# Strassen's scheme for y @ w2_in: the reads of a PSUM bank are given out after both products of the bank

## Chip, cores and metric

One Trainium2 chip, one of its cores. The metric is the device time of one execution in microseconds; the median of the runs is compared.

## What is computed

The input goes through an attention with a small state (its result is called x below, 4352 rows of 512), then through two feed-forward layers. The change touches the second of them only, `_moe2_ref`, with 512 inputs, 2048 hidden columns and 512 outputs per row:

```python
def _moe_ref(x, w_in, w_out, g_ln):
    ...
    return (ln @ w_out)

def _moe2_ref(x, w_in, w_out):
    h = x @ w_in
    r = np.maximum(h, 0.0)
    g = r * r
    return (g @ w_out)

def reference(**kwargs):
    ...
    x = _moe_ref(x=x, **moe_kwargs)          # this result is y below
    return _moe2_ref(x=x, **moe2_kwargs)     # y @ w2_in, relu squared, @ w2_out
```

## The kernel before

Everything is float32. A product of full precision is made of three matmuls (`PASSES`): each operand is split into a high part (a cast to `float32r`) and a rest, and high by high, high by rest and rest by high are added up in PSUM.

**Two phases.** The first does attention and the first feed-forward layer and leaves its result, y, in DRAM. The second, from `p1.close()` on (line 964), does y @ w2_in, the squared relu and the product with w2_out. Its rows come in nine groups j: eight of 512 rows, and the ninth (`j == B`) of 256. For each group, m runs over eight pieces of the hidden dimension, 256 columns each. One pair (j, m) is a step; `emit_l3(j, m)` (line 1010) makes the hidden piece, and `emit_l4(j, m)` (line 1068) multiplies it by w2_out and adds it to four output banks. The loop at line 1096 emits `emit_l3` of a step, the load of the weights of the step after next (`load_wa`), then `emit_l4` of the step before. So TensorE's order is: hidden piece of step i, output part of step i-1, hidden piece of step i+1, output part of step i. In each group from the second on, the output banks of the group before are copied out (`osb`, on ScalarE and VectorE in turn) during its first two steps.

**Strassen's scheme.** For the eight groups of 512 rows, `emit_l3` makes the hidden piece (two by two blocks) from seven products instead of eight, in Winograd's form. `PRODUCTS` (line 23) lists them in the order P1, P6, P2, P7, P5, P3, P4. A product is six matmuls of 256 columns (two k by three passes, `product`, line 1001). Two products share one bank of PSUM (`h2`, a pool of four banks): P1 and P6 the first, P2 and P7 the second, P5 and P3 the third, P4 the fourth alone. Seven reads combine them: a copy `u1` of P1 on ScalarE (`copy`, line 250), and on VectorE (`plus`, line 985) `u2 = u1 + P6`, `c11 = u1 + P2`, `u3 = u2 + P7`, `u4 = u2 + P5`, `c22 = u3 + P5`, `c12 = u4 + P3`, `c21 = u3 - P4`. The four c blocks are the tile `r`. `squares` (line 989) then squares (`L993`, VectorE), casts (`L250`, ScalarE) and subtracts (`L256`, VectorE) each half of r into the tile `g`, which `emit_l4` reads. The ninth group uses no such scheme: it makes its blocks straight, 24 matmuls to one bank, and one read of the full bank.

**What sets the order.** Each engine takes its instructions in the order in which the program emits them. A planner, `Flow`, decides at emission when a read goes out: `fl.pe(cost, ...)` advances a modelled time before every three matmuls, and `fl.poll` emits those waiting tasks whose operands the model holds to be ready. So a read spawned behind P1 goes out between the two k of P6. The framework orders accesses to a tile by their order of emission, and here a tile of PSUM is a whole bank: a read emitted after some matmuls of the bank waits for all of them, and matmuls of the same bank emitted behind the read wait for the read.

**Beside this, early in the second phase,** w2_out is still being decoded: 512 KB loads (`raw`, a ring of three), a conversion on ScalarE (`L300`), two operations on VectorE (`L303`, `L306`), then the split into `wb`, with its cast on ScalarE and its subtraction on GpSimd or VectorE (`L256`). In the fifth to eighth step of each group, y of the next group is loaded and split for the seven products (`yt`, `sy`). All loads and stores are issued by SP in program order; `load_wa` is one load of 1792 KB per step into two buffers `wa`.

Of the kernel before, what the change touches and what calls it, by code (L numbers as in the profile page):

```python
# [153 lines left out]
def attn_solu_relu2_kernel(  # L154
# [92 lines left out]
    def copy(out, in_):  # L247
        def emit(e):
            if e == "A":
                nc.scalar.copy(out=out, in_=in_)  # L250
            else:
                eng_of[e].tensor_copy(out=out, in_=in_)
        return emit
# [11 lines left out]
    def one(engs, emit):  # L265

        def gen(f):
            f = yield engs, f, emit
            return f
        return fl.spawn(gen(fl.end + 0.15), 0.0)  # L270
# [703 lines left out]
    def then(engs, emit, *tasks):  # L974

        at = fl.end + 0.15

        def gen():
            yield None, 0.0, lambda: all(t["done"] is not None for t in tasks)
            f = yield engs, max([at] + [t["done"] for t in tasks]), emit  # L980
            return f
        return fl.spawn(gen(), 0.0)

    def plus(out, in0, in1, *tasks, op=ALU.add):
        return then({"V": 0.42}, lambda e: nc.vector.tensor_tensor(  # L985
            out=out, in0=in0, in1=in1, op=op
        ), *tasks)

    def squares(r, g, tasks):

        def gen():
            yield None, 0.0, lambda: all(t["done"] is not None for t in tasks)
            f = yield {"V": 0.69}, max(t["done"] for t in tasks), lambda e: nc.vector.scalar_tensor_tensor(  # L993
                out=r, in0=r, scalar=0.0, in1=r, op0=ALU.max, op1=ALU.mult
            )
            f = yield {"A": 0.62}, f, copy(g[:, 0], r)
            f = yield {"V": 0.69}, f, sub(g[:, 1], r, g[:, 0].bitcast(F32))
            return f
        return fl.spawn(gen(), 0.0)

    def product(ps, j, w, a, waits, first=True, last=True):
        for k in range(2):
            fl.pe(0.36, *waits)
            for i, (x, y) in enumerate(PASSES):
                nc.tensor.matmul(  # L1005
                    out=ps, lhsT=w[:, y, k], rhs=a[:, x, k],
                    start=(first and k == 0 and i == 0), stop=(last and k == 1 and i == 2),
                )

    def emit_l3(j, m):  # L1010
        w = wa.pop((j, m))
        ready = done.pop(("wa", j, m))
        if m == 0:
            fl.mark(done["y", j], fl.end)
        g = gp.tile([P, 2, 2, S], F32R, tag="g", name="g")
        r = gp.tile([P, 2, 2, Q], F32, tag="r", name="r")
        gt[j, m] = g
        if j == B:
            bank_ = ph2.tile([P, 2, Q], F32, tag="h2", name="h2")
            slot = h2_free.pop(0)  # L1020
            for h in range(2):
                for k in range(2):
                    fl.need(done["y", j, k])
                    product(
                        bank_[:, h], j, w[:, W_AT[f"B{k + 1}{h + 1}"]], yt[j, k],
                        (slot, ready, done["y", j, k]), k == 0, k == 1,
                    )
            first = one({"A": 0.57}, lambda e: nc.scalar.activation(  # L1028
                out=r[:, 0], in_=bank_, func=AF.Relu
            ))  # L1030
            h2_free.append(first)
            done["g", j, m] = squares(r[:, 0], g[:, :, :, :Q], [first])
            return
        u1, u2, u3, u4 = (gp.tile([P, Q], F32, tag=n, name=n, bufs=1) for n in ("u1", "u2", "u3", "u4"))
        ps, t, slots = {}, {}, {}
        for n, (p, a, b) in enumerate(PRODUCTS):
            if n % 2 == 0:
                bank_ = ph2.tile([P, 2, Q], F32, tag="h2", name="h2")
                slot = h2_free.pop(0)
            ps[p] = bank_[:, n % 2]  # L1040
            fl.need(done["y", j, a])
            product(
                ps[p], j, w[:, W_AT[b] - 1], yt[j, a],
                (slot, ready, done["y", j, a]),
            )
            if p == "P1":
                t["u1"] = one({"A": 0.34}, copy(u1, ps["P1"]))
            if p == "P6":
                t["u2"] = plus(u2, u1, ps["P6"], t["u1"])
            if p == "P2":  # L1050
                t["c11"] = plus(r[:, 0, 0], u1, ps["P2"], t["u1"])
            if p == "P7":
                t["u3"] = plus(u3, u2, ps["P7"], t["u2"])
            if p == "P5":
                t["u4"] = plus(u4, u2, ps["P5"], t["u2"])
                t["c22"] = plus(r[:, 1, 1], u3, ps["P5"], t["u3"])
            if p == "P3":
                t["c12"] = plus(r[:, 1, 0], u4, ps["P3"], t["u4"])
            if p == "P4":
                t["c21"] = plus(r[:, 0, 1], u3, ps["P4"], t["u3"], op=ALU.subtract)  # L1060
        for users in (("u1", "u2"), ("c11", "u3"), ("u4", "c22", "c12"), ("c21",)):
            h2_free.append([t[u] for u in users])
        done["g", j, m] = [
            squares(r[:, h].rearrange("p i t -> p (i t)"), g[:, :, h], [t[c] for c in cs])
            for h, cs in ((1, ("c12", "c22")), (0, ("c11", "c21")))
        ]
# [29 lines left out]
    for i in range(len(steps) + 1):  # L1096
        if i < len(steps):
            j, m = steps[i]
            if m == 4 and j < B:
                load_y(j + 1)  # L1100
            emit_l3(j, m)
            if i + 2 < len(steps):
                load_wa(*steps[i + 2])
        if i:
            emit_l4(*steps[i - 1])
# [55 lines left out]
```

## Time and profile before

| | us |
|---|---|
| median of 3 runs | 1290.7 |
| lowest, highest | 1290.64, 1294.53 |
| the profiled execution | 1295.02 |
| its span (first to last instruction) | 1292.9 |
| TensorE matmuls busy | 1162.2 (90%) |
| VectorE busy | 743.0 (57%) |
| ScalarE busy | 458.8 (35%) |
| GpSimd busy | 156.0 (12%) |
| the 16 DMA engines | 46% busy, 166 GB/s on average |
| second phase, TensorE's first hidden matmul to that of the ninth group | 426.75 to 1238.39 |

The time of an execution is that from outside, the span that of the instructions; 2.1 us lie around the span. Busy time of an engine is a sum over its instructions; for TensorE neighbouring matmuls overlap, so a stretch in which it never waits is seen by the starts of its matmuls and by missing waits, not by the busy share.

### The profile page before, as it was taken

The page shows a single profiled execution, that of the slowest core. Times are in us where ns is not written, and L with a number is a line of the kernel's source. Part 1 is how long each engine was busy: PE and PEld are TensorE (multiplying, and loading weights), DVE is VectorE, ACT ScalarE, POOL GpSimd, SP SyncE. Part 2 cuts the span into 40 slices and gives each one's busy share as a digit, 9 for nine tenths or more (in the row PEclk, how much of TensorE's full clock was granted, in tenths as well). Part 3 has the DMA queues.
Part 4 walks back from the last instruction along what each step waited for, and adds up shares of the span by engine and source line. Part 5 has one row for each costly group of instructions (what it writes and reads, how often), then busy time and mean ns, then how long its engine had stood idle before and what let it go on. Part 6 is the DMA issues. An engine that isn't in the chain of part 4 may idle for free.

```text
span 1292.9 us, 17901 instructions
## 1 busy us (share of the span) xinstructions
PE 1162.2 (90%) x7144; PEld 954.4 (74%) x7144; DVE 743.0 (57%) x1429; ACT 458.8 (35%) x848; POOL 156.0 (12%) x209
## 2 busy tenths in 40 slices
PE   5799999999999889888889889889888989888898
PEld 1477777777777877777777777778777777777787
DVE  6876887778765776345536445436445545544432
ACT  5866777777655442112112112112112112111112
POOL 1522343442332130000000000000000000000000
PEclk8899999999999999999999989999999999999999
DMA  9223425532464674544444435445354445353343
GB/s 357 85 72 137 152 99 199 197 125 96 152 220 182 229 284 157 193 159 158 165 185 158 159 121 198 142 176 192 126 183 168 171 147 204 121 197 135 142 163 114
DMA packets 42691, 214.02 MB, mean 166 GB/s; under 512 B 4976, under 2 KB 14192, under 8 KB 31344
## 3 DMA queue, kind: packets, MB, share of 16 engines
q1 hardware_dynamic: 42608, 212.88, 46.0%
q8 instruction: 56, 0.92, 0.3%
q14 instruction: 27, 0.22, 0.1%
HBM read 178.26 MB, written 34.60 MB: 165 GB/s over the span
## 4 chain that ended last, share of the span: by engine, by line
PE 61%; DVE 5%; ACT 3%; DMA 2%; issue 2%; POOL 0%; ACTq 0%; SPq 0%; DVEq 0%
PE h L1005 29%; PE o L1078 27%; PE y L682 3%; DVE u L985 2%; ACT u L250 2%; DVE r L985 2%; DMA out<-osb 2%; PE hps L621 1%; DMA raw<-w_in 0%; PE lnTp L647 0%; DMA raw<-w_out 0%; DVE u L586 0%; DVE dec L303 0%; DVE dec L306 0%; DVE lt L656 0%
## 5 line engine op out<-in xcount | busy, mean ns | idle before, releaser
L1005 PE MATMUL h<-yt,wa 128*128 128x256 f32 x2880 | 402.0, 289 | 98.3 <-DVE r L985 36.4
L1005 PEld LDWEIGHTS h<-yt,wa 128*128 128x128 f32 x2880 | 364.8, 191 | 139.1 <-DVE r L985 47.5
L1078 PE MATMUL o<-wb,g 128*128 128x512 f32 x1632 | 385.0, 391 | 0.0
L1078 PEld LDWEIGHTS o<-wb,g 128*128 128x128 f32 x1632 | 302.9, 189 | 60.2
L985 DVE TENSOR_TENSOR u<-u,h 128x256 f32<-128x256 f32 x192 | 80.6, 420 | 275.2 <-PE h L1005 275.0
L250 ACT CAST g<-r 128x512 fp32r<-128x512 f32 x136 | 84.5, 623 | 390.7 <-DVE r L993 390.7
L682 PE MATMUL y<-lt,wo 128*128 128x512 f32 (+1 forms) x864 | 218.0, 393 | 3.1 <-ACT lt L653 2.3
L682 PEld LDWEIGHTS y<-lt,wo 128*128 128x128 f32 x864 | 149.1, 190 | 39.7 <-issue 5.9
L985 DVE TENSOR_TENSOR r<-u,h 128x256 f32<-128x256 f32 x256 | 100.6, 417 | 69.2 <-PE h L1005 69.2
L993 DVE SCALAR_TENSOR_TENSOR r<-r 128x512 f32<-128x512 f32 x136 | 93.0, 690 | 32.5 <-ACT r L1028 29.4
L256 DVE TENSOR_TENSOR g<-r,g 128x512 fp32r<-128x512 f32 x136 | 93.4, 692 | 10.5 <-ACT g L250 6.4
L621 PE MATMUL hps<-sw,aT 128*128 128x512 f32 x368 | 97.5, 413 | 0.2 <-ACT s_sb L356 0.2
L250 ACT COPY u<-h 128x256 f32<-128x256 f32 x64 | 23.8, 372 | 189.3 <-PE h L1005 189.1
L621 PEld LDWEIGHTS hps<-sw,aT 128*128 128x128 f32 x368 | 68.8, 189 | 23.7 <-issue 6.3
L656 DVE SCALAR_TENSOR_TENSOR lt<-lnTp,g_sb,lt 128x512 fp32r<-128x512 f32 (+1 forms) x72 | 51.4, 713 | 26.1 <-ACT lt L653 25.3
L557 DVE TENSOR_REDUCE hm<-hps 128x1 f32<-128x512 f32 x68 | 45.9, 686 | 26.3 <-PE hps L621 20.5
L250 ACT COPY u<-hps 128x512 f32<-128x512 f32 x68 | 39.0, 583 | 41.7 <-DVE hm L557 40.0
L653 ACT ACTIVATE lt<-lnTp,g_sb 128x512 fp32r<-128x512 f32 (+1 forms) x72 | 48.1, 670 | 5.0 <-PE lnTp L647 4.9
L586 DVE SCALAR_TENSOR_TENSOR u<-u,e 128x1024 f32<-128x1024 f32 x34 | 44.4, 1306 | 8.4 <-ACT e L581 8.2
L592 ACT ACTIVATE e<-u,nmu 128x1024 f32<-128x1024 f32 x34 | 39.2, 1152 | 12.6 <-DVE nmu L589 12.6
L647 PE MATMUL lnTp<-ident,u 128*128 128x128 f32 x272 | 41.6, 273 | 1.5 <-DVE a_sb L256 1.4
L581 ACT ACTIVATE e<-u,nmx 128x1024 f32<-128x1024 f32 x34 | 39.2, 1152 | 6.8 <-DVE nmx L574 5.8
(92 smaller groups left out, 840.7 us busy)
## 6 DMA issues: line engine op xcount, KB each, us to landing
wa<-w_d SPq DMA_DIRECT2D x64, 1792.0 KB, 7.3
w_d<-w2s SPq DMA_DIRECT2D x32, 512.0 KB, 2.9
raw<-w_out SPq DMA_DIRECT2D x24, 512.0 KB, 6.2
out<-osb SPq DMA_DIRECT2D x34, 256.0 KB, 5.4
xT<-x_t SPq DMA_DIRECT2D x8, 1024.0 KB, 5.2
xn<-x_n SPq DMA_DIRECT2D x8, 1024.0 KB, 6.4
y_d<-ys SPq DMA_DIRECT2D x16, 512.0 KB, 4.0
raw<-w_in SPq DMA_DIRECT2D x16, 512.0 KB, 5.9
```

The lines of the kernel that those rows point to most:

```text
L250: nc.scalar.copy(out=out, in_=in_)
L256: return lambda e: eng_of[e].tensor_tensor(out=out, in0=in0, in1=in1, op=ALU.subtract)
L557: one({"V": 0.68}, lambda e, c=c, ps=ps: nc.vector.tensor_reduce(out=m2[:, c:c + 1], in_=ps, axis=AX.X, op=ALU.max)),
L586: nc.vector.scalar_tensor_tensor(out=u, in0=u, scalar=1.0, in1=e_, op0=ALU.mult, op1=ALU.mult, accum_out=us)
L621: nc.tensor.matmul(out=ps, lhsT=lhsT(i, k), rhs=rhs(j, k)[:, cs], start=(k == 0 and n == 0), stop=(k == n_k - 1 and n == len(passes) - 1),)
L653: f = yield {"A": 0.1 + nt * 0.143}, f, lambda e: nc.scalar.activation(out=o[:, 0], in_=pf, func=AF.Copy, scale=gk)
L656: f = yield {"V": 0.1 + nt * 0.155}, f, lambda e: nc.vector.scalar_tensor_tensor(out=o[:, 1], in0=pf, scalar=gk, in1=o[:, 0].bitcast(F32), ...
L682: nc.tensor.matmul(out=ps, lhsT=wo[k][:, w, c * P:(c + 1) * P], rhs=o[:, a], start=(k == 0 and i == 0), stop=(k == K1 - 1 and i == 2),)
L985: return then({"V": 0.42}, lambda e: nc.vector.tensor_tensor(out=out, in0=in0, in1=in1, op=op), *tasks)
L993: f = yield {"V": 0.69}, max(t["done"] for t in tasks), lambda e: nc.vector.scalar_tensor_tensor(out=r, in0=r, scalar=0.0, in1=r, op0=ALU. ...
L1005: nc.tensor.matmul(out=ps, lhsT=w[:, y, k], rhs=a[:, x, k], start=(first and k == 0 and i == 0), stop=(last and k == 1 and i == 2),)
L1078: nc.tensor.matmul(out=ops[j][t], lhsT=g[:, a, h, t * P:(t + 1) * P], rhs=wb[m + h * M2][:, w, :], start=(m == 0 and h == 1 and i == 0), s ...
```

## The change

In `emit_l3`, the seven reads are given out at other places of the loop over the products. Before, each was given out right behind the product that it reads. Now `u1` and `u2` are given out behind P6, `u3` and `c11` behind P7, `c22`, `u4` and `c12` behind P3, `c21` behind P4 as before. So all reads of a bank are spawned behind the last matmul to that bank, and within a bank the order of the reads is changed (u3 ahead of c11, c22 ahead of u4). The planned cost of the copy is 0.36 where it was 0.34. Number and kind of instructions are the same; no matmul changes its place among the matmuls.

```diff
-            if p == "P1":
-                t["u1"] = one({"A": 0.34}, copy(u1, ps["P1"]))
+
             if p == "P6":
+                t["u1"] = one({"A": 0.36}, copy(u1, ps["P1"]))
                 t["u2"] = plus(u2, u1, ps["P6"], t["u1"])
-            if p == "P2":
-                t["c11"] = plus(r[:, 0, 0], u1, ps["P2"], t["u1"])
             if p == "P7":
                 t["u3"] = plus(u3, u2, ps["P7"], t["u2"])
-            if p == "P5":
+                t["c11"] = plus(r[:, 0, 0], u1, ps["P2"], t["u1"])
+            if p == "P3":
+                t["c22"] = plus(r[:, 1, 1], u3, ps["P5"], t["u3"])
                 t["u4"] = plus(u4, u2, ps["P5"], t["u2"])
-                t["c22"] = plus(r[:, 1, 1], u3, ps["P5"], t["u3"])
-            if p == "P3":
                 t["c12"] = plus(r[:, 1, 0], u4, ps["P3"], t["u4"])
             if p == "P4":
                 t["c21"] = plus(r[:, 0, 1], u3, ps["P4"], t["u3"], op=ALU.subtract)
```

TensorE, the hidden piece of one step in the second group, before (h_5628, h_5642, h_5657 and h_5672 are its four banks in turn; the square brackets name the engines that a matmul waits for):

```order
L1005 MATMUL h_5628<-yt,wa 128x256 [waits DMAHW1_49]
L1005 MATMUL h_5628<-yt,wa 128x256 x8
L1005 MATMUL h_5628<-yt,wa 128x256 [waits Activation_49]
L1005 MATMUL h_5628<-yt,wa 128x256 x2
L1005 MATMUL h_5642<-yt,wa 128x256 x9
L1005 MATMUL h_5642<-yt,wa 128x256 [waits DVE_49]
L1005 MATMUL h_5642<-yt,wa 128x256 x2
L1005 MATMUL h_5657<-yt,wa 128x256 x9
L1005 MATMUL h_5657<-yt,wa 128x256 [waits DVE_49]
L1005 MATMUL h_5657<-yt,wa 128x256 x2
L1005 MATMUL h_5672<-yt,wa 128x256 x6
```

The same step of the changed kernel (its banks are h_5628, h_5641, h_5656, h_5671):

```order
L1005 MATMUL h_5628<-yt,wa 128x256 [waits DMAHW1_49,DVE_49]
L1005 MATMUL h_5628<-yt,wa 128x256 x11
L1005 MATMUL h_5641<-yt,wa 128x256 [waits DVE_49]
L1005 MATMUL h_5641<-yt,wa 128x256 x11
L1005 MATMUL h_5656<-yt,wa 128x256 [waits DVE_49]
L1005 MATMUL h_5656<-yt,wa 128x256 x11
L1005 MATMUL h_5671<-yt,wa 128x256 [waits DVE_49]
L1005 MATMUL h_5671<-yt,wa 128x256 x5
```

The wait ahead of the tenth matmul of each of the first three banks is gone; instead the first matmul of each bank waits, for the reads of the same bank by the step before.

VectorE, the reads of that step and what follows, before:

```order
L985 TENSOR_TENSOR u_5625<-u_5624,h_5628 128x256 [waits PE_49,Activation_49]
L985 TENSOR_TENSOR r<-u_5624,h_5642 128x256 [waits PE_49]
L985 TENSOR_TENSOR u_5626<-u_5625,h_5642 128x256 [waits DVE_49,PE_49]
L985 TENSOR_TENSOR u_5627<-u_5625,h_5657 128x256 [waits PE_49]
L985 TENSOR_TENSOR r<-u_5626,h_5657 128x256 [waits DVE_49,PE_49]
L985 TENSOR_TENSOR r<-u_5627,h_5657 128x256 [waits DVE_49]
L993 SCALAR_TENSOR_TENSOR r<-r 128x512 [waits DVE_49]
L985 TENSOR_TENSOR r<-u_5626,h_5672 128x256 [waits PE_49]
L993 SCALAR_TENSOR_TENSOR r<-r 128x512 [waits DVE_49]
L256 TENSOR_TENSOR g<-r,g 128x512 [waits Activation_49] x2
```

And of the change:

```order
L985 TENSOR_TENSOR u_5625<-u_5624,h_5628 128x256 [waits Activation_49]
L985 TENSOR_TENSOR u_5626<-u_5625,h_5641 128x256 [waits DVE_49,PE_49]
L985 TENSOR_TENSOR r<-u_5624,h_5641 128x256
L985 TENSOR_TENSOR r<-u_5626,h_5656 128x256 [waits DVE_49,PE_49]
L985 TENSOR_TENSOR u_5627<-u_5625,h_5656 128x256
L985 TENSOR_TENSOR r<-u_5626,h_5671 128x256 [waits PE_49]
L985 TENSOR_TENSOR r<-u_5627,h_5656 128x256 [waits DVE_49]
L993 SCALAR_TENSOR_TENSOR r<-r 128x512 [waits DVE_49] x2
L256 TENSOR_TENSOR g<-r,g 128x512 [waits Activation_49] x2
```

One wait for TensorE per bank is left; c21 (of the fourth bank, h_5671) now stands ahead of c12, and both squarings behind the two of them.

ScalarE at the start of the second phase, before (u_4575 and u_4643 are the copies u1 of the first two steps, raw the pieces of w2_out):

```order
L250 COPY u_4575<-h_4579 128x256 [waits PE_49]
L300 ACTIVATE dec<-raw 128x512 [waits DMAHW1_49]
L300 ACTIVATE dec<-raw 128x512 [waits DMAHW2_49,Activation_49]
L250 COPY u_4643<-h_4647 128x256 [waits DVE_49,PE_49,Activation_49]
L250 CAST g<-r 128x512 [waits DVE_49]
L300 ACTIVATE dec<-raw 128x512 [waits DMAHW3_49,Pool_49]
```

And of the change:

```order
L250 COPY u_4575<-h_4579 128x256 [waits PE_49]
L300 ACTIVATE dec<-raw 128x512 [waits DMAHW1_49]
L300 ACTIVATE dec<-raw 128x512 [waits DMAHW2_49,Activation_49]
L300 ACTIVATE dec<-raw 128x512 [waits DMAHW3_49,Pool_49]
L250 COPY u_4641<-h_4645 128x256 [waits DVE_49,PE_49,Activation_49]
L250 CAST g<-r 128x512 [waits DVE_49] x2
```

The third decode, with its wait for a load, now stands ahead of the copy of the second step and of both casts of the first.

## Rows read from the trace of the kernel before

**Rows 1.** Waits, 426.7 to 1238.4 us: waiter, releaser, us in total, times, longest.
```profile
PE h L1005 <- DVE r L985: 36.4, 55, 1.8
PE h L1005 <- ACT u L250: 33.7, 64, 1.1
PE h L1005 <- DVE u L985: 28.3, 55, 0.5
```

**Rows 2.** Timeline of one step: start us, us, engine, line, instruction, [idle before <-releaser].
```profile
816.23 1.23 PE L1005 MATMUL h<-yt,wa 128*128 128x256 f32 x9
...
817.98 1.69 PE L1005 MATMUL h<-yt,wa 128*128 128x256 f32 x12 [0.52 <-ACT u L250]
...
820.18 1.70 PE L1005 MATMUL h<-yt,wa 128*128 128x256 f32 x12 [0.51 <-DVE r L985]
...
822.39 1.33 PE L1005 MATMUL h<-yt,wa 128*128 128x256 f32 x9 [0.51 <-DVE u L985]
...
823.56 5.63 PE L1078 MATMUL o<-wb,g 128*128 128x512 f32 x24
...
825.50 1.46 DVE L256 TENSOR_TENSOR g<-r,g 128x512 fp32r<-128x512 f32 x2
...
829.03 1.23 PE L1005 MATMUL h<-yt,wa 128*128 128x256 f32 x9
```

**Rows 3.** Timeline, TensorE alone, a step with two waits, to the next's start.
```profile
791.41 1.23 PE L1005 MATMUL h<-yt,wa 128*128 128x256 f32 x9
...
796.80 1.34 PE L1005 MATMUL h<-yt,wa 128*128 128x256 f32 x9 [0.51 <-DVE u L985]
...
803.44 1.23 PE L1005 MATMUL h<-yt,wa 128*128 128x256 f32 x9
```

**Rows 4.** Timeline, TensorE alone, a step with one wait, to the next's start.
```profile
484.00 1.23 PE L1005 MATMUL h<-yt,wa 128*128 128x256 f32 x9
485.69 4.22 PE L1005 MATMUL h<-yt,wa 128*128 128x256 f32 x33 [0.46 <-ACT u L250]
...
495.22 1.23 PE L1005 MATMUL h<-yt,wa 128*128 128x256 f32 x9
```

**Rows 5.** Timeline, TensorE alone, the ninth group's first step and the second's start.
```profile
1238.39 3.04 PE L1005 MATMUL h<-yt,wa 128*128 128x256 f32 x24
1241.27 5.63 PE L1078 MATMUL o<-wb,g 128*128 128x512 f32 x24
1246.73 3.04 PE L1005 MATMUL h<-yt,wa 128*128 128x256 f32 x24
```

**Rows 6.** Timeline, TensorE alone, the second phase's first hidden and first output matmuls.
```profile
426.75 1.24 PE L1005 MATMUL h<-yt,wa 128*128 128x256 f32 x9
...
439.83 2.46 PE L1078 MATMUL o<-wb,g 128*128 128x512 f32 x10
```

**Rows 7.** Timeline, ScalarE alone, the first two decodes of that phase.
```profile
431.51 0.67 ACT L300 ACTIVATE dec<-raw 128x512 f32<-128x512 f32 x1 [3.11 <-DMA raw<-w_out]
433.44 0.68 ACT L300 ACTIVATE dec<-raw 128x512 f32<-128x512 f32 x1 [1.26 <-DMA raw<-w_out]
```

**Rows 8.** Windows: stretch, length, busy us (instructions) of PE PEld DVE ACT POOL, PEclk, DMA share, GB/s.
```profile
426.70:532.80 106.10, 94.37 (x572) 82.49 (x572) 73.26 (x138) 36.30 (x65) 17.62 (x13) 1.00 0.64 231
532.80:634.80 102.00, 89.52 (x530) 77.38 (x529) 50.75 (x101) 18.00 (x33) 0.00 (x0) 1.00 0.46 165
...
736.80:841.80 105.00, 92.42 (x530) 79.80 (x529) 50.74 (x101) 18.00 (x33) 0.00 (x0) 0.97 0.45 160
...
1238.40:1288.60 50.20, 50.20 (x312) 45.34 (x311) 12.38 (x18) 11.42 (x19) 0.00 (x0) 1.00 0.43 147
```

**Rows 9.** Tile wa, loads of 427 to 1238 us, from issue to landing.
```profile
DMA to landing us min/median/max: 5.0/7.3/8.8
```

**Rows 10.** Timeline, second step of the sixth group: a wait behind the output copies.
```profile
947.42 0.69 DVE L252 COPY osb<-o 128x512 f32<-128x512 f32 x1 [5.27 <-PE h L1005]
...
948.82 1.69 PE L1005 MATMUL h<-yt,wa 128*128 128x256 f32 x12 [1.79 <-DVE r L985]
```

## The prediction

> **What bounds the kernel now.** I read the waits of the second phase first. TensorE's hidden matmuls wait 174 times, 98.4 us in all, and every time for a read of PSUM: 64 times for the copy u1, 55 for an r block (mostly c11), 55 for a u (u4) [rows 1]. The groups of output matmuls never wait. Then the timeline of a common step [rows 2]: TensorE runs nine matmuls, stands idle 0.52 us for ScalarE, runs twelve, idle 0.51 for VectorE, twelve, idle 0.51, then nine and the 24 output matmuls without a gap. The breaks lie where the order puts the waits, ahead of the tenth matmul of a bank: P1's or P2's or P5's read goes out in the middle of the bank's second product, waits for the nine matmuls so far, and the last three wait for it. In the steady steps nothing else ends a wait of TensorE, so the phase is TensorE's time plus these waits.
>
> **What one wait costs** is more than its idle time, since matmuls overlap and a restart is slow. The trace has its own experiment, steps in which the planner happened to give out fewer reads in mid-bank. From the start of one step to the next: three waits 829.03 - 816.23 = 12.80 us [rows 2], two waits 803.44 - 791.41 = 12.03 (ScalarE's stands in the line left out) [rows 3], one wait 495.22 - 484.00 = 11.22 [rows 4]. That is 0.77 to 0.81 per wait, and puts a step without waits near 10.45.
>
> **What a step without waits costs**, independently: the ninth group reads only full banks and has no wait. There 24 hidden matmuls take 1241.27 - 1238.39 = 2.88 us, 0.120 each, and 24 output matmuls 1246.73 - 1241.27 = 5.46 us [rows 5]. A Strassen step has 42 and 24: 42 x 0.120 + 5.46 = 10.50. The two ways agree, and I take 10.50.
>
> The Trainium skill, "TensorE: Matmul & The Clock Gate" (Wait — 56ns, not 53.3ns?), has back-to-back matmuls start N ÷ 2.4 GHz + 2.5 ns apart, which gives estimates of 109 ns for 256 columns and 216 ns for 512. By these a step would take 9.77 us, and the sum below would be 47 us lower. The rows say 120 and 228 ns in a stretch with no wait at all at a granted clock of 1.00, so the measurement decides.
>
> **The change, part by part.**
>
> *Removed: the waits in mid-bank.* In the order of the changed kernel every bank of the eight Strassen groups is written in one piece, so all 174 go. The phase runs from 426.75 [rows 6] to 1238.39 [rows 5], 811.6 us, and holds 64 hidden pieces and 63 output parts. Without waits: 64 x 42 x 0.120 + 63 x 5.46 = 322.6 + 344.0 = 666.6. Gain 145.0. The other way: 174 waits at 0.77 are 134.0; in the second step of the seven later groups one wait is some 1.1 longer (1.79 idle where 0.5 is usual, VectorE being held in the output copies [rows 10]), 7 to 8 us; and one group took 105.0 where its neighbour took 102.0, at a granted clock of 0.97 [rows 8], 3.0 us. Together 144 to 145.
>
> *Added: waits at the start of a bank*, for the reads of that bank in the step before. In the change VectorE reads two blocks behind the last product, c21 of the fourth bank and c12 of the third. Now the step's last subtraction ends at 825.50 + 1.46 = 826.96, 3.4 us after the hidden piece's end at about 823.56 [rows 2]. The reads, two squarings, two casts and two subtractions are the same in number, so I take the same 3.4. The next writer of the third bank comes 5.46 + 24 x 0.120 = 8.3 us after the piece's end; that of the first comes 5.46 us after it, and its reads are the oldest. So this costs nothing. A wait that is met already costs nothing either: in the order before, the step of one wait [rows 4] has such waits at two bank starts, and its length fits the others. If VectorE fell more than 7 us behind, the cover would be gone and the third bank would be late.
>
> *g for the output part.* It is needed 5.46 + 5.04 = 10.5 us after its hidden piece ends, and is done after 3.4. Nothing, except in the first step, where no output part lies between: there the two hidden pieces end at 426.75 + 84 x 0.120 = 436.8. ScalarE now has a third decode ahead of the casts of g. The first two loads end their waits at 431.51 and 433.44 [rows 7]; at the same spacing the third comes at 435.4. Decode 0.67, copy, two casts and one subtraction give about 438.3, so the first output part waits 1.5 us. Bounds: 0, if the third load lands with the second, and 3.0, if the output part starts where it does now, 439.83 [rows 6]. I take 1.5, worked out from the nearest rows.
>
> *Moved on the queues.* SP has the same 72 loads of wa, later w2_out loads by a place or two. A load of wa is issued when a hidden piece ends and is needed two steps on: 2 x 10.5 - 5.04 = 16 us of cover against 7.3 us in the median and 8.8 at most [rows 9]. Bytes per time rise by 811.6 / 666.6: from 165 GB/s to 201 in a common group, from 231 to about 281 in the first, DMA share 0.64 to about 0.78 [rows 8]. Hidden; were the cover gone, wa would be late next. VectorE's share rises from 50.75 / 102.0 to 50.75 / 84.0 = 60%, in the first group from 73.26 / 106.1 to 82% [rows 8]. Late next is VectorE in the first group.
>
> *The output copies of a group* hold VectorE until 948.1 in the sixth group [rows 10]; they remain, but what stands behind them is now read late without stopping TensorE: the bank is written to its end and its next writer is a step away. The 1.1 us each go with the waits.
>
> **Sum.** The profiled execution took 1295.0, 4.3 above the median; 3.0 of this I put on the stretch at the lower clock, which need not be in the median run. Against the profile: 1295.0 - 145.0 + 1.5 = 1151.5. Against the median, without gaining the 3.0 twice: 1290.7 - 142.0 + 1.5 = 1150.2. Forecast 1150.
>
> **The rivals.**
> - *The first group becomes bound by VectorE and ScalarE.* It lasts 106.1 now; its floor is 9 x 5.04 + 8 x 5.46 = 89.0. VectorE's 73.3 us would fill 82%, in an order where it also waits for decodes and loads. If none of the 17.1 is gained: 1167. For it, the two engines' in-order waits; against it, no wait of TensorE's on w2_out now and 10 us of cover for g.
> - *The waits behind the output copies stay*, moved to bank starts: seven times 1.1 us, 1158. Against it, 8 us of cover there.
> - *TensorE drops to the lower clock.* Without pauses its load rises. At 1.2 instead of 2.4 GHz work takes twice as long; 145 us are lost from 22% of the 667 us on. With a quarter at 1.2: 1150 + 167 = 1317, slower than before. For it, one stretch at 0.97; against it, 50 us at 100% busy and a granted clock of 1.00 in the ninth group [rows 8].
> - *The matmuls start closer together* once nothing interrupts them for long, at most one column per cycle of the upper level: 256 / 2.4 = 107 ns and 512 / 2.4 = 213 ns instead of 120 and 228. That is 64 x 42 x 0.013 + 63 x 24 x 0.015 = 58 us more, 1092. The 24 and 24 undisturbed ones [rows 5] speak against it. The rule of the Trainium skill's page named above would make it 1103 as an estimate.
> - *The change does not do what it says*: the reads still cut banks, or bank starts wait as long as mid-bank did: 1291. The order shows otherwise.
>
> **How the numbers follow.** Forecast 0.72 (1146 to 1155, by the bounds of the first stall and the 3 us of clock), first group 0.12, output copies 0.10, closer matmuls 0.03, lower clock 0.015, no effect 0.015. The range 1145 to 1167 takes in the first three. Differences of under 0.3% are about what a measurement of this kernel cannot tell from none; faster has 0.97, same 0.015, slower 0.015.
>
> **What would show it.** In the profile after: PE h waits for r, u and u1 gone, the step's period 10.5 us, one wait of one to three us ahead of the first output part, wa and g never named as releasers in the later groups, PEclk 1.00. Wrong it would be if bank starts show waits for DVE in common steps, if the step stays above 11 us, or if PEclk falls below 0.97.

## The result, and the profile after

The changed kernel takes 1150.74 us (median of 4 runs, 1149.48 to 1151.89) where the kernel before, in the same comparison, takes 1290.67: ratio 0.8911, interval [0.8889, 0.8933], 139.9 us less. The prediction was 1150. The profiled execution took 1151.89, its span is 1149.7.

The page of the kernel after, the row of the hidden matmuls and the shares of the chain that ended last (out<-in, count | busy, mean ns | idle before):

```profile
PE 67%; DVE 1%; ACT 0%; DMA 0%; issue 0%; POOL 0%; SPq 0%; DVEq 0%; ACTq 0%
...
L1005 PE MATMUL h<-yt,wa 128*128 128x256 f32 x2880 | 356.6, 283 | 0.0
```

The 98.4 us of TensorE's waits [rows 1] are 0.0, all of them. The timeline of TensorE alone, at the start of the second phase, in the second step of the sixth group, and at the ninth group:

```profile
428.94 10.24 PE L1005 MATMUL h<-yt,wa 128*128 128x256 f32 x84
439.02 5.63 PE L1076 MATMUL o<-wb,g 128*128 128x512 f32 x24
444.48 1.72 PE L1005 MATMUL h<-yt,wa 128*128 128x256 f32 x13
...
853.98 5.20 PE L1005 MATMUL h<-yt,wa 128*128 128x256 f32 x42
859.02 5.63 PE L1076 MATMUL o<-wb,g 128*128 128x512 f32 x24
864.48 1.72 PE L1005 MATMUL h<-yt,wa 128*128 128x256 f32 x13
...
1095.48 3.04 PE L1005 MATMUL h<-yt,wa 128*128 128x256 f32 x24
```

What was four pieces with three breaks [rows 2] is one row of 42 matmuls, then 24 output matmuls: 864.48 - 853.98 = 10.50 us. Every step from 444.48 to 1095.48 has this length, (1095.48 - 444.48) / 62 = 10.50. The phase went from 811.6 to 1095.48 - 428.94 = 666.5 us, 145.1 less. Of the span's remainder, the part ahead of the phase is 2.2 us longer, 428.94 instead of 426.75, with the same TensorE instructions in the same order: windows of 260 to 280 us of both kernels (before first) show the granted clock there. In the fourteen traces of this case the second phase starts at 426.0 to 430.9 us, so this differs from one execution to the next and is not the change's doing.

```profile
260.00:280.00 20.00, 18.75 (x97) 15.38 (x96) 17.78 (x37) 15.84 (x30) 7.55 (x13) 1.00 0.17 66
```

```profile
260.00:280.00 20.00, 18.17 (x87) 14.66 (x87) 16.27 (x34) 15.61 (x29) 6.45 (x11) 0.91 0.18 69
```

The end after the ninth group's start is 54.3 us (54.5 before). So 145.1 - 2.2 + 0.2 = 143.1, which is 1295.02 - 1151.89. The same windows as in [rows 8], now 89.0 and 84.0 us long:

```profile
428.90:517.90 89.00, 89.00 (x572) 81.37 (x571) 71.60 (x138) 35.51 (x65) 17.19 (x13) 1.00 0.76 275
517.90:602.00 84.10, 84.10 (x531) 76.39 (x530) 48.82 (x101) 17.82 (x33) 0.00 (x0) 1.00 0.56 202
```

TensorE is busy in every microsecond, at a granted clock of 1.00. VectorE's share is 80% in the first group and 58% in the next (forecast 82% and 60%), the DMA share in the first group 0.76 (forecast 0.78), the rate in the next 202 GB/s (forecast 201). A load of wa lands after 7.2 us in the median and 9.6 at most (7.3 and 8.8 before [rows 9]).

### The profile page after: what moved, and what is told of

Its sections match the earlier page's. It is cut to its first block, busy times and chain, and to the rows that moved or that the text cites. A ratio compares the mean times of both kernels' runs of the same rounds, so it can differ in the third digit from the quotient of the medians.

```text
span 1149.7 us, 17914 instructions
## 1 busy us (share of the span) xinstructions
PE 1116.0 (97%) x7144; PEld 943.9 (82%) x7144; DVE 727.9 (63%) x1429; ACT 457.5 (40%) x848; POOL 155.4 (14%) x209
## 4 chain that ended last, share of the span: by engine, by line
PE 67%; DVE 1%; ACT 0%; DMA 0%; issue 0%; POOL 0%; SPq 0%; DVEq 0%; ACTq 0%
PE o L1076 32%; PE h L1005 30%; PE y L682 3%; PE hps L621 1%; DMA raw<-w_in 0%; PE lnTp L647 0%; DVE u L586 0%; DVE lt L656 0%; POOL wb L256 0%; DVE hm L557 0%; ACT e L581 0%; DVE u L610 0%; ACT u L250 0%; ACT lt L653 0%; DVE yt L256 0%
## 5 line engine op out<-in xcount | busy, mean ns | idle before, releaser
L1005 PEld LDWEIGHTS h<-yt,wa 128*128 128x128 f32 x2880 | 354.9, 192 | 5.5
L1005 PE MATMUL h<-yt,wa 128*128 128x256 f32 x2880 | 356.6, 283 | 0.0
L993 DVE SCALAR_TENSOR_TENSOR r<-r 128x512 f32<-128x512 f32 x136 | 89.6, 697 | 29.3 <-ACT r L1028 29.3
L621 PE MATMUL hps<-sw,aT 128*128 128x512 f32 x368 | 98.4, 416 | 1.0 <-ACT s_sb L356 1.0
L256 DVE TENSOR_TENSOR g<-r,g 128x512 fp32r<-128x512 f32 x136 | 88.3, 688 | 14.5 <-ACT g L250 11.2
L653 ACT ACTIVATE lt<-lnTp,g_sb 128x512 fp32r<-128x512 f32 (+1 forms) x72 | 48.2, 671 | 5.4 <-PE lnTp L647 5.3
L592 ACT ACTIVATE e<-u,nmu 128x1024 f32<-128x1024 f32 x34 | 39.2, 1153 | 12.7 <-DVE nmu L589 12.7
L581 ACT ACTIVATE e<-u,nmx 128x1024 f32<-128x1024 f32 x34 | 39.2, 1153 | 6.8 <-DVE nmx L574 5.8
```

The costliest lines, as they stand in the source:

```text
L256: return lambda e: eng_of[e].tensor_tensor(out=out, in0=in0, in1=in1, op=ALU.subtract)
L621: nc.tensor.matmul(out=ps, lhsT=lhsT(i, k), rhs=rhs(j, k)[:, cs], start=(k == 0 and n == 0), stop=(k == n_k - 1 and n == len(passes) - 1),)
L653: f = yield {"A": 0.1 + nt * 0.143}, f, lambda e: nc.scalar.activation(out=o[:, 0], in_=pf, func=AF.Copy, scale=gk)
L1005: nc.tensor.matmul(out=ps, lhsT=w[:, y, k], rhs=a[:, x, k], start=(first and k == 0 and i == 0), stop=(last and k == 1 and i == 2),)
```

## The experiments

Every run was compared with the kernel before on its own chip, where that took 1292.9 to 1294.8 us. "Over the floor" below is the sum over the 63 step lengths of what a step takes beyond 10.50 (15.55 for the first two together), from the starts of the hidden pieces in the trace; the kernel before has 145.1, the change 0.0.

**One read put back, on ScalarE.** The copy u1 behind P1 again:

```diff
+            if p == "P1":
+                t["u1"] = one({"A": 0.36}, copy(u1, ps["P1"]))
             if p == "P6":
-                t["u1"] = one({"A": 0.36}, copy(u1, ps["P1"]))
```

> The changed kernel with one read put back: the copy u1 is given out right behind P1 again, so in 57 of the 64 Strassen steps it cuts the first bank. Theory (each read that cuts a bank costs TensorE about 0.78 us, idle and restart together, and nothing else changed): 57 x 0.78 = 44 us above 1150.7, about 1195 us; the steps with it 11.28 us, PE h waits for ACT u in the trace 57 times at 0.5 us each, and none for DVE. Rival (the gain comes from the new order or spacing of the reads on VectorE, which stays here): about 1151.

Measured: 1197.36 us, ratio 0.9261 [0.9246, 0.9276]; over the floor 45.3. Waits of TensorE, and a common step with the start of the next:

```profile
PE h L1005 <- ACT u L250: 31.1, 57, 1.7
```

```profile
535.43 1.23 PE L1005 MATMUL h<-yt,wa 128*128 128x256 f32 x9
537.18 4.21 PE L1005 MATMUL h<-yt,wa 128*128 128x256 f32 x33 [0.52 <-ACT u L250]
...
546.70 1.23 PE L1005 MATMUL h<-yt,wa 128*128 128x256 f32 x9
```

The step is 11.27 us, 0.77 above 10.50, though the idle row says 0.52. So the rule "one cut, 0.77 us" holds for this read alone, and 57 cuts give 43.9 of the 45.3.

**One bank's reads put back, on VectorE.** c22 and u4 behind P5 again:

```diff
+            if p == "P5":
+                t["c22"] = plus(r[:, 1, 1], u3, ps["P5"], t["u3"])
+                t["u4"] = plus(u4, u2, ps["P5"], t["u2"])
             if p == "P3":
-                t["c22"] = plus(r[:, 1, 1], u3, ps["P5"], t["u3"])
-                t["u4"] = plus(u4, u2, ps["P5"], t["u2"])
```

> The changed kernel with the reads of P5 (c22 and u4) given out behind P5 again: in 58 steps c22 cuts the third bank, on VectorE. Theory: 58 x 0.78 = 45 us, about 1196 us, waits of PE h for DVE r 58 times at 0.5 us. Rival (VectorE's waits cost more than ScalarE's, since reads queue there): above 1205. Rival (order on VectorE is what counts): about 1151.

Measured: 1211.8 us, ratio 0.9367 [0.9351, 0.9383]: 16 more than my theory had it. Over the floor 62.1. The common step is 11.27 us here too, so the price of a cut is the same for ScalarE's read and for VectorE's where the engine is not late. The rest stands in two places: the second steps of the seven later groups have 17.3 over the floor where seven cuts would have 5.4, and the first group has one long wait. That wait, all engines, VectorE being busy with the decoding of w2_out (`L303`, `L306`, `wb`):

```profile
465.68 4.11 PE L1005 MATMUL h<-yt,wa 128*128 128x256 f32 x33
...
469.99 1.63 DVE L306 SCALAR_TENSOR_TENSOR dec<-raw,dec 128x512 int32<-128x512 int32 x1
...
471.55 0.68 DVE L256 TENSOR_TENSOR wb<-dec,wb 128x512 fp32r<-128x512 f32 x1
...
473.00 0.74 DVE L985 TENSOR_TENSOR r<-u,h 128x256 f32<-128x256 f32 x2
...
473.80 2.29 PE L1005 MATMUL h<-yt,wa 128*128 128x256 f32 x9 [4.00 <-DVE r L985]
```

A read that cuts a bank hands TensorE whatever VectorE is late by.

**A bank for each product.** The reads stand where the kernel before has them, but no product shares its bank:

```diff
-            if n % 2 == 0:
-                bank_ = ph2.tile([P, 2, Q], F32, tag="h2", name="h2")
-                slot = h2_free.pop(0)
-            ps[p] = bank_[:, n % 2]
+            bank_ = ph2.tile([P, 2, Q], F32, tag="h2", name="h2")
+            slot = h2_free.pop(0)
+            ps[p] = bank_[:, 0]
```

(The list of freed banks is filled behind each product instead of at the end.)

> The kernel before, its reads where they were, each given out behind its own product; but each product gets a bank of its own (the same pool of four banks, half of each used), so that a read never shares a bank with matmuls that are still to come. Theory (what stops TensorE is the sharing of a bank between a read and later matmuls, not that reads are given out early): no waits in mid-bank, a bank is written again three products later, 2.16 us, against about 0.9 us that a read needs; steps of 10.50 us and 1149 to 1153 in all. Rival (reads given out early stop TensorE by themselves, or four banks for seven products are too few): 1200 to 1290, with waits at the banks' first matmuls.

Measured: 1160.32 us, ratio 0.8972 [0.8957, 0.8987]. Common steps are 10.50 us. So giving a read out early costs nothing by itself; what cost was the sharing of a bank with matmuls still to come. But the theory's 1149 to 1153 is 7 to 11 us short: over the floor 8.8, of which 7.1 in the second steps of the later groups.

**The order within a bank.** The two other edits undone:

```diff
-                t["u1"] = one({"A": 0.36}, copy(u1, ps["P1"]))
+                t["u1"] = one({"A": 0.34}, copy(u1, ps["P1"]))
...
-                t["u3"] = plus(u3, u2, ps["P7"], t["u2"])
-                t["c11"] = plus(r[:, 0, 0], u1, ps["P2"], t["u1"])
+                t["c11"] = plus(r[:, 0, 0], u1, ps["P2"], t["u1"])
+                t["u3"] = plus(u3, u2, ps["P7"], t["u2"])
...
-                t["c22"] = plus(r[:, 1, 1], u3, ps["P5"], t["u3"])
                 t["u4"] = plus(u4, u2, ps["P5"], t["u2"])
+                t["c22"] = plus(r[:, 1, 1], u3, ps["P5"], t["u3"])
```

> The changed kernel with the two other edits undone: c11 ahead of u3 and u4 ahead of c22, as before, and the planned cost of the copy 0.34 again; all reads still behind the full bank. Theory (these two edits are worth nothing): 1149 to 1153, steps of 10.50 us. Rival (part of the gain is theirs): 1160 or more.

Measured: 1149.7 us, ratio 0.8894 [0.8881, 0.8908]; over the floor 0.0. These edits are worth nothing.

**Two banks instead of four.** `bufs=2` for `ph2`, and the list of freed banks filled behind each bank.

> The changed kernel with two banks for the hidden products instead of four. Theory (the waits at a bank's start are covered by a wide margin): the third bank is the first again, whose two reads are done some 1.0 us after it is full, while the second bank takes 1.44 us to write; so TensorE does not wait, or only by the 0.1 to 0.3 us by which a read can be late: 1150 to 1165. Rival (the cover of several us that four banks give is needed): 1180 or more, with waits of PE h for DVE in each step.

Measured: 1174.83 us, ratio 0.9079 [0.906, 0.9098]: between theory and rival. The common step is 10.50 us, so two banks do cover the reads there. Over the floor 23.7: 9.6 in the first group, 12.3 in the second steps of the later groups. Such a second step with two banks, the sixth group's, and the same place in the change with four:

```profile
870.73 3.03 PE L1005 MATMUL h<-yt,wa 128*128 128x256 f32 x24
...
874.30 0.69 DVE L252 COPY osb<-o 128x512 f32<-128x512 f32 x1 [4.42 <-PE h L1005]
874.91 0.94 DVE L985 TENSOR_TENSOR u<-u,h 128x256 f32<-128x256 f32 x2
875.38 2.41 PE L1005 MATMUL h<-yt,wa 128*128 128x256 f32 x18 [1.61 <-DVE u L985]
```

```profile
853.98 5.20 PE L1005 MATMUL h<-yt,wa 128*128 128x256 f32 x42
...
857.58 0.69 DVE L252 COPY osb<-o 128x512 f32<-128x512 f32 x1 [4.44 <-PE h L1005]
858.18 0.94 DVE L985 TENSOR_TENSOR u<-u,h 128x256 f32<-128x256 f32 x2
```

In both, the group's fourth output copy, VectorE's second, starts 3.6 us into the hidden piece and the reads come behind it. With two banks TensorE has filled both by then and stands; with four it goes on. The bracket names a matmul of `h` as what the copy waited for, which can't be: the copy reads an output bank. The order has it wait for a store as well, since `osb` has three buffers and a group four copies. In the trace of the change the same wait is put down to the store in three of the seven groups and to `h` in four:

```profile
DVE osb L252 <- PE h L1005: 17.5, 4, 4.6
DVE osb L252 <- DMA out<-osb: 13.5, 3, 4.6
```

**Ten more operations on VectorE per step**, on a scratch tile:

```diff
+        for _ in range(10):
+            one({"V": 0.4}, lambda e: nc.vector.tensor_scalar(
+                out=idle_, in0=idle_, scalar1=1.0, scalar2=None, op0=ALU.mult
+            ))
```

> The changed kernel with ten more operations of VectorE in each Strassen step (a scratch tile multiplied by one), some 3.5 to 4.5 us a step, mostly in between the reads. Theory (the reads are 7 us or more off TensorE's path, and VectorE, at 5.5 of 10.5 us in a common step, has room): common steps stay at 10.50 us; only the first group, where VectorE's work was 8.1 us a step, is bound by VectorE and loses 10 to 25 us: 1160 to 1175. Rival (TensorE follows VectorE closely in all groups): 64 x 4 us, 1300 to 1400.

Measured: 1219.53 us, ratio 0.9433 [0.9407, 0.9459]; neither. Over the floor 69.0: 20.1 in the first group, as foretold, and 48.2 in the first steps of the seven later groups, 6.9 each, where I had expected nothing. A window of later steps, and the output part in such a step (lines are shifted by the edit):

```profile
596.00:680.00 84.00, 79.68 (x498) 72.03 (x497) 75.06 (x170) 16.60 (x32) 0.00 (x0) 0.98 0.51 185
```

```profile
982.53 0.69 DVE L256 TENSOR_TENSOR g<-r,g 128x512 fp32r<-128x512 f32 x1
983.13 4.57 DVE L1064 TENSOR_SCALAR idle__4565<-idle__4565 128x512 f32<-128x512 f32 x10
983.47 0.63 PE L1082 MATMUL o<-wb,g 128*128 128x512 f32 x2
987.62 0.68 DVE L256 TENSOR_TENSOR g<-r,g 128x512 fp32r<-128x512 f32 x1
...
988.36 7.70 PE L1082 MATMUL o<-wb,g 128*128 128x512 f32 x22 [4.27 <-DVE g L256]
```

The ten take 4.57 us, and VectorE is busy 75.06 of 84 us. Most steps still run at 10.50; but the steps that split y put VectorE further behind: the last subtraction of g comes 8.0 us after its hidden piece in a common step and 9.4 in the seventh of a group, and the cover is some 11. In the last step of six of the seven groups concerned the ten then stand in VectorE's order between the two subtractions of g (982.53 and 987.62 above), where in the other steps of the later groups they stand ahead of both or behind both. Without them in between, the second subtraction would have ended at about 983.8 (an estimate: two of 0.6 to 0.7 us from 982.53 on), just ahead of the third output matmul, which needs it; with them TensorE waits 4.27 us, for g rather than for a bank. (At the start of the second group it waits 3.42 us for `yt` instead.) 22 matmuls then take 7.70 us instead of some 5.2: the granted clock was 0.50 from 988.4 to 993.5. So VectorE's room is real, but smaller than its mean share tells, and what an added operation costs depends on its place in the order.

**One bank.** `bufs=1`:

> The changed kernel with a single bank for the hidden products: every bank must be read before the next one is written. Theory: three uncovered read-outs a step (two reads of 0.4 us with 0.1 us of signalling and a restart of 0.27: about 1.2 us each, the third bank's three reads about 1.4), the fourth covered by the output part: 3.8 us a step, 64 x 3.8 = 243 above 1150.7, about 1394. That is slower than the kernel before (1290.7), which waits for one read at a time. Rival (the wait is as long as before, one read each): 1150.7 + 192 x 0.78 = 1300.

Measured: 1487.02 us (2 runs), ratio 1.1492 [1.1456, 1.1529]. A common step:

```profile
533.58 1.59 PE L1005 MATMUL h<-yt,wa 128*128 128x256 f32 x12
536.14 1.69 PE L1005 MATMUL h<-yt,wa 128*128 128x256 f32 x12 [0.97 <-DVE u L985]
538.67 1.69 PE L1005 MATMUL h<-yt,wa 128*128 128x256 f32 x12 [0.84 <-DVE r L985]
541.66 0.98 PE L1005 MATMUL h<-yt,wa 128*128 128x256 f32 x6 [1.30 <-DVE r L985]
...
547.94 1.24 PE L1005 MATMUL h<-yt,wa 128*128 128x256 f32 x9
```

It takes 547.94 - 533.58 = 14.36 us to the next one's start, 3.86 above 10.50; I had 3.8. The 93 us by which the total missed lie elsewhere: some 35 us in the second and 30 in the fifth steps of the later groups and the rest mostly in the first group. VectorE has other work there that nothing covers (output copies, the splitting of y, the decoding of w2_out), and the mean granted clock is 0.959 in this trace; how the 93 divide between the two was not tried. So the change gains only with banks to go on with: the read-out of a full bank is longer than that of a product.

**A fourth buffer for `osb`** (`bufs=4` in the pool `op`), in four kernels: before, the change, two banks, a bank per product.

> The kernel before with a fourth buffer for the output copies (osb), so that VectorE's second copy of a group no longer waits for a store. Theory (in the second step of the seven later groups this wait is passed on to TensorE, because a read that cuts a bank stands behind the copy): seven times 1.0 to 1.1 us, 7 to 8 us, and with it the pause of 1.8 us after which the granted clock fell once: 1281 to 1287 against 1290 to 1293. The second steps then take 12.8 us like the others. Rival (VectorE is held by something else there): no change.

> The changed kernel with the fourth buffer for osb. Theory (VectorE is still held there, but nothing of TensorE waits for it): no change, 1149 to 1152. Rival: faster by several us.

> Two banks for the hidden products, as in e5_two_banks, with the fourth buffer for osb. Theory (of the 23.7 us that two banks cost over steps of 10.50 us, 12.3 stand in the second steps of the later groups and come from VectorE's wait for a store, 9.6 in the first group from the decoding of w2_out, the rest from the splitting of y): 1174.8 - 12 = 1163, second steps 10.50 us. Rival (with two banks the copies themselves are enough to make the reads late): above 1170.

> A bank per product with the reads where they were before, as in e3_bank_per_product, with the fourth buffer for osb. Theory (7.1 of its 8.8 us over steps of 10.50 us come from the same wait for a store): 1160.3 - 7 = 1153, within 0.3% of the changed kernel. Rival (a bank per product is worse by itself): 1158 or more.

| kernel | three buffers | four | ratio to before, four | second steps over the floor, three to four |
|---|---|---|---|---|
| before | 1292.92 | 1284.73 | 0.9943 [0.9926, 0.9961] | 26.4 to 16.1 |
| the change | 1150.74 | 1150.60 | 0.8902 [0.8885, 0.8919] | 0.0 to 0.0 |
| two banks | 1174.83 | 1161.87 | 0.8992 [0.8969, 0.9014] | 12.3 to 0.0 |
| a bank per product | 1160.32 | 1152.56 | 0.8918 [0.89, 0.8936] | 7.1 to 0.0 |

The four times with four buffers and the 1292.92 were taken side by side; the other times with three buffers are from the comparisons described above. All four came out as the theory had them. (The 26.4 of the kernel before hold the 3.0 of its one stretch at the lower clock.) With two banks and four buffers the sixth group's second step is one piece again:

```profile
873.98 5.20 PE L1005 MATMUL h<-yt,wa 128*128 128x256 f32 x42
879.01 1.32 PE L1078 MATMUL o<-wb,g 128*128 128x512 f32 x5
```

A bank per product comes to within 0.2% of the change: two ways to the same floor.

**The cut on VectorE, with the fourth buffer.**

> The changed kernel with the reads of P5 behind P5 again, as in e2_third_bank_behind_p5, and a fourth buffer for osb. Theory (e2 came out 16 us above its 1196 because VectorE, held by a store in the second steps, was late for the read that cuts the bank, in seven groups, and the granted clock fell after three of the long waits): the second steps take 11.27 us like the others, 1211.8 - 12 = 1200. What is left above 1196 is one wait of some 4 us in the first group. Rival (a cut by VectorE costs more than one by ScalarE in every step): 1205 or more.

Measured: 1202.92 us, ratio 0.929 [0.9269, 0.9312]. The second steps went from 17.3 to 5.4 over the floor, as expected. 50.8 are left in all, with 8.7 in the first group; that wait was there again (3.60 us idle) behind the same decoding, and its cause is read from the trace, it was not taken away. The theory's 1200 is 3 us short.

## Why the prediction was right

- **Mid-bank waits are the bound, and all go.** Right: 98.4 us idle became 0.0, and putting back one read, or one bank's, brings back one wait a step of 0.77 us.
- **A step costs 10.50 without waits.** Right to the second decimal, from 24 hidden and 24 output matmuls of the ninth group that nothing disturbed [rows 5]. The Trainium skill's spacing, N ÷ 2.4 GHz + 2.5 ns ("TensorE: Matmul & The Clock Gate", Wait — 56ns, not 53.3ns?), would make it 9.77, an estimate; the trace after disagrees over 64 steps, with 42 matmuls in 859.02 - 853.98 = 5.04 us, 120 ns each.
- **A wait costs more than its idle time.** Right: 0.77 against 0.52, in every variant with one cut.
- **Bank starts are covered.** Right for four banks, and with two to spare in common steps. Where I priced the cover of the output copies it was right too: 1.1 us each go in the change (0.0 over the floor), and their cause, a store that VectorE waits for, is shown by the fourth buffer.
- **The stall of the first output part, 1.5 us.** Wrong: none. The output matmuls follow the 84 hidden ones at 439.02 without idle time. Two steps of this term failed. One is the third load: I spaced it like the second and had its decode 8.7 us into the phase, and in the trace after it starts 7.3 us in. The other is what TensorE needs: I had the first output matmul wait for a subtraction behind both casts. In the order only the third output matmul waits for the second subtraction, which ends at 439.07, while that matmul starts at about 439.5. Had the load come 1.3 us later, as I had it, the wait would by these lines have been some 0.9 us (an estimate), not 1.5. The lower bound, 0, was in the range, but for a reason that did not come: the third load did not land with the second.

```profile
434.81 0.67 ACT L300 ACTIVATE dec<-raw 128x512 f32<-128x512 f32 x1 [0.99 <-DMA raw<-w_out]
...
436.28 0.69 ACT L300 ACTIVATE dec<-raw 128x512 f32<-128x512 f32 x1 [0.81 <-DMA raw<-w_out]
...
437.78 1.29 DVE L256 TENSOR_TENSOR g<-r,g 128x512 fp32r<-128x512 f32 x2
```

- **VectorE as the bound of the first group** did not come: 80% busy and no wait of TensorE, as the sum had it. But it came nearer than the sum knew. The 3.4 us that I took from a hidden piece's end to its last subtraction became 3.5 in a common step and up to 10.0 in the first group. The piece that ends at 481.02 there, in the trace after:

```profile
481.02 5.63 PE L1076 MATMUL o<-wb,g 128*128 128x512 f32 x24
...
486.48 5.20 PE L1005 MATMUL h<-yt,wa 128*128 128x256 f32 x42
...
487.24 0.74 DVE L985 TENSOR_TENSOR r<-u,h 128x256 f32<-128x256 f32 x2
...
489.71 1.28 DVE L256 TENSOR_TENSOR g<-r,g 128x512 fp32r<-128x512 f32 x2
...
491.52 1.32 PE L1076 MATMUL o<-wb,g 128*128 128x512 f32 x5
```

Its second subtraction ends at 490.99, and the third output matmul that needs it starts at about 491.98: 1.0 us of cover is left out of 11. Its last reads end at 487.98, and the next writer of the third bank starts at 486.48 + 24 x 0.120 = 489.36, 1.4 us later. The experiment with ten more operations shows what is behind that: the first group lost 20 us at once.

- **The lower clock** did not come: 1.00 in all windows of the phase. It came in variants where TensorE stood for 1.9 us and more at a time (two banks, c22 and u4 behind P5, ten more operations, one bank).

The sum against the median, 1290.7 - 142.0 + 1.5 = 1150.2, ended 0.5 us below the 1150.74: the stall that was not there makes up for some 2 us by which the gain of the medians, 139.9, lies below 142.0. In the profiled executions the two can be told apart: no stall, and 2.2 us more ahead of the phase, at the lower clock. That they nearly cancel is luck; the 145 of the waits is not.

The wait was on a whole bank because the framework orders accesses by bank. The Trainium skill, "PSUM — Partial Sum Buffer" (PSUM bank collisions raise a hardware error), says to guard PSUM by bank and quadrant (32 of the 128 partitions), not by address. By that rule a guard of the half that is read was no way out, since both products of a bank lie on the same 128 partitions. No run here shows a collision; the bank per product shows that reads of one bank need not stop the writing of another: its common steps are 10.50 us.

## What to carry to other kernels

Where two accumulations share a PSUM bank and accesses are ordered by bank, a read between them stops the matmuls until it is done, here 0.77 us each time and more when the reader is late; give reads out when the bank is full, or give each accumulation its own bank, and have enough banks that the reader may be late by its worst delay, not its usual one. Price a wait by the lengths of steps that have it and steps that don't, not by its idle row. An engine held elsewhere, as VectorE by a ring one buffer too short, costs nothing while cover is left (0.0 in the change) and shows when the cover is cut (12.3 us with two banks): look for it before cutting buffers.

## What the runs showed that I had not expected

A wait that is met costs TensorE nothing measurable: after the change up to four stand in every step, and the steps are those of the floor. Matmuls start 120 ns apart at 256 columns and 228 at 512, 13 and 14 ns more than 256 and 512 columns divided by 2.4 GHz, also in 667 us without a pause; what these nanoseconds are was not tried.

The granted clock was 1.00 over the whole phase with TensorE 100% busy. In the second phase of the kernel before it fell once, to half, right behind a long pause:

```profile
742.09 2.08 PE L1005 MATMUL h<-yt,wa 128*128 128x256 f32 x12 [1.76 <-DVE r L985]
```

```profile
743.15:749.98 6.83, 6.32 (x23) 5.34 (x22) 4.20 (x9) 1.25 (x2) 0.00 (x0) 0.50 0.31 80
```

Behind the six other pauses of 1.3 to 1.8 us of that phase, and behind the usual ones of 0.5, it stayed at 1.00, so the pause alone does not tell when it falls. With the fourth buffer for `osb` these seven pauses are gone and the kernel before has 1.00 over its whole second phase too.
